# Operand steps at the two pass changes of an expert stage, moved behind the next unit's weight parts, and a larger filling budget at one point

## The chip, the cores and the metric

The kernel runs on one core of a Trainium2 chip. The metric is the time of one execution on the device in microseconds (us); shorter is better. Engines are named as in the profile: PE (matrix), PEld (its weight loads), DVE (vector), ACT (scalar), POOL (GpSimd), SP (issues the DMAs). Each engine works through its own instructions in the order in which the program wrote them.

## What is computed

Three stages follow one another; the output of each is the input of the next.

```python
attn_out = _attn_ref(q, k, v, phi)            # batch 4, 8 heads, 576 positions, 64 wide; 32 memory slots
x = attn_out.transpose(0, 2, 1, 3).reshape(2304, 512)
# second stage, d_ff = 2048
h = x @ w_in
x = (h * np.clip(h + 3.0, 0.0, 6.0) / 6.0) @ w_out
# third stage, the experts: E = 4, F = 1024
p = domain_probs / (domain_probs.sum(-1, keepdims=True) + 1e-09)
for e in range(E):
    h = np.maximum(x @ w1[e], 0.0)
    out += p[:, e:e + 1] * (h @ w2[e])
```

## The kernel before

**Number format.** Each float32 operand of a large product is held as two fp32r parts, `hi` (an ACT cast) and `lo` (a DVE subtraction of `hi` from the source). A product is three matmuls, hi·hi, hi·lo and lo·hi (`PASSES`). The second matmul of such a triple is the first that reads the `lo` part of the operand that is streamed, the third the first that reads the `lo` of the other.

**Before the expert stage.** Attention and the second stage are ordered by a planner (`Plan`), which runs until about 394 us of the trace. The change reaches it in one place only: the operand steps of the first token pair (`x_ops(0)`) are part of its plan, as a chain in the order of the list that `x_ops` returns.

**The expert stage** is written out by hand, at the end of `body`. The 2304 tokens are six tiles of 384; a pass `p` (0 to 2) takes two tiles. In a pass, chunk `c` (0 to 7) is one expert and half of its 1024 hidden columns; `n = 8p + c` counts 24 chunks. For a chunk, `unit(n, 0)` and `unit(n, 1)` compute the hidden activations of both tiles, 256 columns each, and `second(n, 1)` and `second(n, 0)` multiply them by the second weights of the expert, in three blocks of 128 tokens each, and add the result to `oacc` on DVE (line 961; line 959 in a pass's first chunk). In a pass's last chunk each `oacc` block is stored by a DMA.

**A unit** (`m = 2n + u`) does its 2×2 block product with seven products instead of eight, so it needs sums of the blocks of both sides: of the weights and of the tokens. The products run on PE in the order b, a, c, d, a, c, d (the second a, c and d add to the PSUM bank of the first, and are called a', c', d' here), six matmuls of 128x384 each. After the first b, ACT copies the bank (`p6`, line 914). DVE then forms `u2` from bank a and `p6`, `u4` from bank c and `u2`, and so on (line 905). So a' cannot start until `u2` has read bank a, nor c' until `u4` has read bank c. ACT applies relu (line 878), DVE the `lo` of the result (line 879).

**Weight parts.** For each unit a DMA brings a raw tile `u_raw`. Its steps, in order: casts `hi0`, `hi3` (ACT), `lo0`, `lo3` (DVE), four sums in place in the raw tile `s1`, `s3`, `s2`, `s4` (POOL, lines 326 to 335), then casts `hi2`, `hi1` of the summed blocks, and `lo2`, `lo1`. In the rows below W16_1 is part 1 of unit 16. Product b reads part 1, a part 0, c part 2, d part 2; a' part 0, c' part 1, d' part 3. The second weights have steps `w2hi` and `w2lo`, four of each per chunk (w2_8_3 is part 3 of chunk 8); `second` uses them in the order 0, 2, 3, 1.

**Token operands.** For each pass, `x_ops(p)` makes seven operands from the two token tiles: X11, X22, X21 are blocks, XT1 to XT4 differences. That is seven ACT casts of 128x768 (line 683), four DVE subtractions in place (line 689) and seven DVE `lo` steps (line 686). They overwrite the operands of the pass before, so they come after the last unit of that pass. Product b reads XT2 (xop4), a X11 (xop0), c XT1 (xop3), d XT3 (xop5), a' X21 (xop1), c' X22 (xop2), d' XT4 (xop6).

**What sets the order.** All these preparing steps stand in one list, `todo`, in a fixed order with marks called gaps. At given points the stage takes steps from its front:

```python
    def fill(t):            # takes steps until t us of vector work are used, or until a gap
    def need(key):          # takes steps until the one named has been taken
```

In a unit, `step(0.6)` stands after products b and a, and `step(0)` after the others; `second` calls `fill(1.9)` after each of its six blocks. Only DVE steps count against the budget, at fixed costs (0.6 for a 512 wide `lo`, 0.86 for an operand step); casts, sums and loads cost nothing there. A wait of one step holds everything behind it on its engine. At the two pass changes (after chunks 7 and 15, called seams here) the 18 operand steps are inserted at the front of `todo` before the second products of the old pass's last chunk.

Of the kernel before, what the change touches and what calls it, by code (L numbers as in the profile page):

```python
# [17 lines left out]
B, H, S, D = 4, 8, 576, 64  # L18
# [108 lines left out]
def body(ctx: ExitStack, tc: tile.TileContext, phiT, kv, qT, w_in, w_out, w1, w2, dp, out):  # L127
# [19 lines left out]
    at = ExitStack()  # L147
# [10 lines left out]
    def bank(name):  # L158
        return ps_w.tile([P, 512], F32, tag="h", name=name)
# [421 lines left out]
    for t in range(NTT):  # L581
        p, r = t * TW, []
        while p < (t + 1) * TW:
            b, s0 = divmod(p, S)
            n = min(S - s0, (t + 1) * TW - p)
# [79 lines left out]
    X11, X21, X22, XT1, XT2, XT3, XT4 = range(7)  # L665
    xop = {}

    def x_tile(k):
        if k not in xop:
            pool, tag = {X11: (0, "x0"), X21: (0, "x1"), X22: (0, "x2"), XT1: (0, "x3"), XT3: (wip, "wia"),  # L670
                         XT2: (keep_a, "attnT0"), XT4: (keep_a, "attnT1")}[k]
            xop[k] = (pool or late["x"]).tile([P, 2, 2, TW], F32R, tag=tag, name=f"xop{k}")
        return xop[k]

    def x_ops(p):

        a, b = acc[2 * p] if 2 * p in acc else None, acc.get(2 * p + 1)
        B11, B21 = (lambda: acc[2 * p][:, 0:2]), (lambda: acc[2 * p][:, 2:4])
        B12, B22 = (lambda: acc[2 * p + 1][:, 0:2]), (lambda: acc[2 * p + 1][:, 2:4])
        v = nc.vector.tensor_tensor  # L680

        def hi(k, src):
            nc.scalar.copy(x_tile(k)[:, 0], src())

        def lo(k, src):
            v(out=x_tile(k)[:, 1], in0=src(), in1=x_tile(k)[:, 0].bitcast(F32), op=ALU.subtract)

        def sub(out, x, y):
            v(out=out(), in0=x(), in1=y(), op=ALU.subtract)

        H = lambda k, src: (f"xhi{k}", "A", 750, partial(hi, k, src))
        L = lambda k, src: (f"xlo{k}", "V", 860, partial(lo, k, src))
        D = lambda k, out, x, y: (f"xt{k}", "V", 860, partial(sub, out, x, y))
        return [H(X11, B11), H(X22, B22), H(X21, B21), L(X11, B11), L(X22, B22), D(1, B11, B12, B11),
                D(3, B12, B22, B12), D(2, B22, B22, B11), H(XT1, B11), H(XT2, B22), H(XT3, B12), L(X21, B21),
                L(XT1, B11), L(XT2, B22), L(XT3, B12), D(4, B21, B21, B22), H(XT4, B21), L(XT4, B21)]

    def plan_ffn():
        nu = [(c, b) for c in range(NC1) for b in range(B)]
# [37 lines left out]
        for name, eng, cost, fn in x_ops(0):  # L737
            op((name,), eng, cost, fn, *prev)
            prev = [(name,)]
# [21 lines left out]
    todo, made = [], set()  # L761
# [4 lines left out]
    def go():  # L766
        key, t, ok, fn = todo.pop(0)
        assert ok(), key
        fn()
        made.add(key)  # L770
        return t

    def fill(t):
        some = False
        while todo and t > 0 and todo[0][2]():
            if todo[0][0] == "gap":
                todo.pop(0)
                if some:
                    break
            else:  # L780
                t -= go()
                some = True

    def need(key):
        while key not in made:
            if todo[0][0] == "gap":
                todo.pop(0)
            else:
                go()
# [79 lines left out]
    def flush(keep):  # L869
        while len(late_lo) > keep:  # L870
            late_lo.pop(0)()

    def h_tile(n, f, half, src):

        k = h_free.pop(0)
        h = hpool.tile([P, 2, TW], F32R, tag=f"h{k}", name=f"h{n}_{f}_{half}")
        hts[n, f, half] = h, k
        nc.scalar.activation(h[:, 0], src, AF.Relu)  # L878
        late_lo.append(lambda: nc.vector.scalar_tensor_tensor(out=h[:, 1], in0=src, scalar=0.0, in1=h[:, 0].bitcast(F32),
                                                              op0=ALU.max, op1=ALU.subtract))  # L880

    def unit(n, u):
        m = 2 * n + u
        W = units[m]
        bk = {}
        tmp = {}

        def tmp_tile(name, tag):
            tmp[name] = wip.tile([P, TW], F32, tag=tag, name=f"{name}_{m}")
            return tmp[name]  # L890

        def prod(b, k, o, x, first, last):
            if first:
                bk[b] = bank(f"p{b}")[:, 0:TW]
            for kt in range(2):
                for i, (xx, y) in enumerate(PASSES):
                    nc.tensor.matmul(bk[b], W[k][0][:, xx, o, kt * P:(kt + 1) * P], xop[x][:, y, kt],  # L897
                                     start=first and kt == 0 and i == 0, stop=kt == 1 and i == 2,
                                     skip_group_check=not first)

        def c_tile(tag):
            return rawp.tile([P, TW], F32, tag=tag, name=f"{tag}_{m}", bufs=2)

        def add_to(out, b, x):
            nc.vector.tensor_tensor(out=out, in0=bk[b], in1=x, op=ALU.add)  # L905
            return out

        def step(t):
            flush(1)
            fill(t)  # L910

        need(("lo1", m))
        prod("b", 1, 0, XT2, True, True)
        nc.scalar.copy(tmp_tile("p6", "wi0"), bk["b"])  # L914
        step(0.6)
        need(("lo0", m))
        prod("a", 0, 0, X11, True, False)
        add_to(tmp_tile("u2", "wi1"), "a", tmp["p6"])
        step(0.6)
        need(("lo2", m))  # L920
        prod("c", 2, 0, XT1, True, False)
        add_to(tmp_tile("u4", "wi2"), "c", tmp["u2"])
        step(0)
        prod("d", 2, 1, XT3, True, False)
        h_tile(n, u + 2, 1, add_to(c_tile("cy"), "d", tmp["u4"]))
        step(0)
        prod("a", 0, 1, X21, False, True)
        h_tile(n, u, 0, bk["a"])
        step(0)
        prod("c", 1, 1, X22, False, True)  # L930
        h_tile(n, u, 1, add_to(c_tile("cx"), "c", tmp["u2"]))
        step(0)
        need(("lo3", m))
        prod("d", 3, 0, XT4, False, True)
        h_tile(n, u + 2, 0, add_to(c_tile("cx"), "d", tmp["u2"]))
        step(0)
        for k, (_, t) in units.pop(m).items():
            (free_half if k == 3 else free_slots).append(t)

    def second(n, half):  # L940
# [26 lines left out]
        if half == 0:  # L967
            for i in range(4):
                free_slots.append(w2s.pop((n, i))[1])

    for n in range(last_n + 1):
        p, c = divmod(n, NCE)
        unit(n, 0)
        unit(n, 1)
        if c == NCE - 1 and p + 1 < NP:
            flush(0)
            for name, eng, cost, fn in reversed(x_ops(p + 1)):
                todo.insert(0, ((name, p + 1), cost / 1e3 if eng == "V" else 0, yes, fn))
        second(n, 1)
        second(n, 0)  # L980
        if c == NCE - 1 and p + 1 < NP:
            need((f"xlo{XT4}", p + 1))
# [33 lines left out]
```

## Time and profile before

| | |
|---|---|
| median of 3 runs | 1158.57 us (1158.21 to 1161.49) |
| the profiled execution | 1160.18 us, its span 1158.40 us |
| PE, PEld busy | 97%, 89% |
| DVE, ACT, POOL busy | 71%, 40%, 13% |
| mean granted TensorE clock | 0.994 of full speed |
| expert stage | from 394.2 us of the span to its end |
| HBM traffic | 83.66 MB read, 4.72 MB written |

Times in the rows are microseconds from the start of the span. A row of the timeline is one instruction or several of the same form in a row (xN), with its start and its length; what stands in brackets is the idle time of the engine before it, and what ended that. The end of a matmul is modelled, so of PE the starts are compared. The span is 1.78 us shorter than the execution's own time, and that execution is 1.61 us above the median of the runs.

### The profile page before, as it was taken

How to read it: one execution, taken by the hardware profiler on the slowest of the kernel's cores; microseconds unless marked ns; L12 is line 12 of the kernel's file. 1: busy time of each engine (PE TensorE's matmuls, PEld its weight loads, DVE VectorE, ACT ScalarE, POOL GpSimd, SP SyncE). 2: the span in 40 equal slices, each digit the busy share in tenths (PEclk: the TensorE clock that was granted, in tenths of full speed). 3: DMA queues.
4: the chain of work that ended last, by engine and by line, in shares of the span. 5: the costliest groups of instructions: out<-in, count | busy, mean ns of one | idle time of the engine just before them, and what ended most of it. 6: DMA issues, size and time to landing. Idle time of an engine off the chain costs nothing. (4 is left out here: it accounts for less than half of the span.)

```text
span 1158.4 us, 16603 instructions
## 1 busy us (share of the span) xinstructions
PE 1123.4 (97%) x6488; PEld 1027.2 (89%) x6488; DVE 821.6 (71%) x1510; ACT 463.4 (40%) x918; POOL 150.3 (13%) x200
## 2 busy tenths in 40 slices
PE   4899999999999999999999899999999899999998
PEld 3799999999999989999999799999999799999997
DVE  6999899974568577666667766666667766666664
ACT  2666654433344333333333343333334433333321
POOL 0000000000011023211121222222210222222210
PEclk9999999999999999999999999999999999999999
DMA  9832231210000032221111321222220222221201
GB/s 362 296 112 97 77 106 57 90 37 1 1 19 1 11 105 86 73 74 56 64 63 54 110 91 55 73 73 74 73 74 28 100 91 73 73 72 56 73 1 55
DMA packets 31167, 89.46 MB, mean 77 GB/s; under 512 B 2928, under 2 KB 2928, under 8 KB 30576
## 3 DMA queue, kind: packets, MB, share of 16 engines
q1 hardware_dynamic: 31088, 88.39, 22.6%
q8 instruction: 51, 0.84, 0.3%
q14 instruction: 28, 0.23, 0.1%
HBM read 83.66 MB, written 4.72 MB: 76 GB/s over the span
## 5 line engine op out<-in xcount | busy, mean ns | idle before, releaser
L953 PE MATMUL po<-w,h 128*128 128x512 f32 x1728 | 396.8, 390 | 1.4 <-DVE w L355 1.4
L953 PEld LDWEIGHTS po<-w,h 128*128 128x128 f32 x1728 | 323.9, 188 | 68.2 <-DVE w L355 1.8
L648 PE MATMUL pacc<-g,w 128*128 128x384 f32 x1152 | 213.9, 337 | 0.9 <-DVE g L372 0.9
L648 PEld LDWEIGHTS pacc<-g,w 128*128 128x128 f32 x1152 | 198.9, 188 | 8.0 <-issue 5.9
L961 DVE SCALAR_TENSOR_TENSOR oacc<-po,pr,oacc 128x512 f32<-128x512 f32 x126 | 94.3, 748 | 113.6 <-PE po L953 113.6
L326 POOL TENSOR_TENSOR u_raw<-u_raw 128x256 f32<-128x256 f32 x48 | 36.2, 755 | 954.1 <-DVE pair L323 690.8
L320 ACT CAST W<-u_raw 128x512 fp32r<-128x512 f32 (+1 forms) x160 | 87.5, 599 | 155.0 <-POOL u_raw L329 127.3
L897 PE MATMUL pa<-xop,W 128*128 128x384 f32 x576 | 116.5, 336 | 7.2 <-DVE u L905 7.2
L622 PE MATMUL ph<-attnT,u 128*128 128x384 f32 (+1 forms) x768 | 121.3, 306 | 0.1
L622 PEld LDWEIGHTS ph<-attnT,u 128*128 128x128 f32 x768 | 112.4, 190 | 5.9 <-DVE g L372 1.7
L897 PE MATMUL pc<-xop,W 128*128 128x384 f32 x576 | 116.7, 337 | 0.0
L897 PEld LDWEIGHTS pa<-xop,W 128*128 128x128 f32 x576 | 102.1, 189 | 7.8 <-DVE u L905 7.8
L897 PEld LDWEIGHTS pc<-xop,W 128*128 128x128 f32 x576 | 102.5, 190 | 0.1
L323 DVE TENSOR_TENSOR W<-u_raw,W 128x512 fp32r<-128x512 f32 (+1 forms) x160 | 97.5, 661 | 1.2 <-ACT W L320 0.9
L878 ACT ACTIVATE h<-cx 128x384 fp32r<-128x384 f32 x96 | 50.5, 526 | 79.1 <-DVE cx L905 79.1
L369 ACT CAST g<-t 128x384 fp32r<-128x384 f32 x96 | 49.4, 514 | 78.5 <-PE pacc L648 69.7
L372 DVE TENSOR_TENSOR g<-t,g 128x384 fp32r<-128x384 f32 x96 | 53.1, 555 | 38.3 <-ACT g L369 38.1
L914 ACT COPY p<-pb 128x384 f32<-128x384 f32 x48 | 23.1, 481 | 141.8 <-PE pb L897 141.5
L897 PE MATMUL pd<-xop,W 128*128 128x384 f32 x384 | 77.7, 337 | 0.0
L628 ACT ACTIVATE t<-ph,three 128x384 f32<-128x384 f32 x96 | 55.9, 582 | 52.9 <-DVE g L372 44.0
L897 PEld LDWEIGHTS pd<-xop,W 128*128 128x128 f32 x384 | 68.4, 190 | 0.0
L355 DVE TENSOR_TENSOR w<-w2raw,w 128x512 fp32r<-128x512 f32 x96 | 65.1, 703 | 0.0
(92 smaller groups left out, 1204.9 us busy)
## 6 DMA issues: line engine op xcount, KB each, us to landing
u_raw<-in_w SPq DMA_DIRECT2D x48, 512.0 KB, 3.2
w2raw<-in_w SPq DMA_DIRECT2D x48, 512.0 KB, 3.4
raw<-in_w_in SPq DMA_DIRECT2D x16, 512.0 KB, 4.0
kv<-in_kv SPq DMA_DIRECT2D x16, 512.0 KB, 7.7
raw<-in_w_out SPq DMA_DIRECT2D x16, 512.0 KB, 3.3
q<-in_qT SPq DMA_DIRECT2D x4, 1152.0 KB, 6.8
out_y<-oacc SPq DMA_DIRECT2D x18, 256.0 KB, 2.0
phi<-in_phiT SPq DMA_DIRECT2D x4, 576.0 KB, 8.6
```

The source lines that it names most:

```text
L320: nc.scalar.copy(w[:, 0], r()[:, slice(*parts[k])])
L323: v(out=W[k][0][:, 1], in0=r()[:, slice(*parts[k])], in1=W[k][0][:, 0].bitcast(F32), op=ALU.subtract)
L355: nc.vector.tensor_tensor(out=w[:, 1], in0=w2raw[n, q // 2][:, q % 2], in1=w[:, 0].bitcast(F32), op=ALU.subtract)
L369: nc.scalar.copy(hi, src)
L372: nc.vector.tensor_tensor(out=lo, in0=src, in1=hi.bitcast(F32), op=ALU.subtract)
L622: nc.tensor.matmul(ps[:, o:o + m], uts[c, b][:, x, hq, i * P:(i + 1) * P], attnT[b][:, y, hq, s0:s0 + m], start=(k == 0), stop=(k == 5))
L628: nc.scalar.activation(t, st["ph", n], AF.Relu, bias=three, scale=1.0)
L648: nc.tensor.matmul(pacc[j][:, 0:TW], w[:, x, j * P:(j + 1) * P], g[:, y], start=(i == 0 and k == 0), stop=(i == NI - 1 and k == 2))
L878: nc.scalar.activation(h[:, 0], src, AF.Relu)
L897: nc.tensor.matmul(bk[b], W[k][0][:, xx, o, kt * P:(kt + 1) * P], xop[x][:, y, kt], start=first and kt == 0 and i == 0, stop=kt == 1 and i ...
L953: nc.tensor.matmul(ps, hts[n, i, half][0][:, x, j * P:(j + 1) * P], w2s[n, i][0][:, y], start=(i == 0 and k == 0), stop=(i == 1 and k == 2))
L961: nc.vector.scalar_tensor_tensor(out=o, in0=ps, scalar=sc, in1=o, op0=ALU.mult, op1=ALU.add)
```

## The change

Four edits, all in the expert stage but for the list that the planner also uses:

- In `x_ops` the operand XT2 is made before XT1 (cast and `lo`), and the fourth subtraction and the cast of XT4 come before the `lo` of XT3.
- In a unit, the point after product b takes `step(1.2)` instead of `step(0.6)`.
- One `fill(0.1)` stands ahead of the stage's first unit.
- At a seam the 18 operand steps are inserted not at the front of `todo` but behind the step `s4` of unit 2n + 3, if that is still in the list: behind the last weight parts of the next chunk's first unit, and the first parts and the POOL sums of its second unit.

```diff
@@ x_ops
         return [H(X11, B11), H(X22, B22), H(X21, B21), L(X11, B11), L(X22, B22), D(1, B11, B12, B11),
-                D(3, B12, B22, B12), D(2, B22, B22, B11), H(XT1, B11), H(XT2, B22), H(XT3, B12), L(X21, B21),
-                L(XT1, B11), L(XT2, B22), L(XT3, B12), D(4, B21, B21, B22), H(XT4, B21), L(XT4, B21)]
+                D(3, B12, B22, B12), D(2, B22, B22, B11), H(XT2, B22), H(XT1, B11), H(XT3, B12), L(X21, B21),
+                L(XT2, B22), L(XT1, B11), D(4, B21, B21, B22), H(XT4, B21), L(XT3, B12), L(XT4, B21)]
@@ unit
         nc.scalar.copy(tmp_tile("p6", "wi0"), bk["b"])
-        step(0.6)
+        step(1.2)
         need(("lo0", m))
@@ the stage's loop
+    fill(0.1)
     for n in range(last_n + 1):
         p, c = divmod(n, NCE)
         unit(n, 0)
         unit(n, 1)
         if c == NCE - 1 and p + 1 < NP:
             flush(0)
-            for name, eng, cost, fn in reversed(x_ops(p + 1)):
-                todo.insert(0, ((name, p + 1), cost / 1e3 if eng == "V" else 0, yes, fn))
+
+            at = max([0] + [k + 1 for k, x in enumerate(todo) if x[0] == ("s4", 2 * n + 3)])
+            todo[at:at] = [((name, p + 1), cost / 1e3 if eng == "V" else 0, yes, fn) for name, eng, cost, fn in x_ops(p + 1)]
         second(n, 1)
         second(n, 0)
```

**DVE at the first seam, beginning of the second products of chunk 7.** The first row is the accumulation of the first of their six blocks. Before:

```order
L961 SCALAR_TENSOR_TENSOR oacc1_4437<-po_6391,pr_105,oacc1_4437 128x512
L686 TENSOR_TENSOR xop0_3815<-acc2_1331,xop0_3815 128x768
L686 TENSOR_TENSOR xop2_3838<-acc3_1555,xop2_3838 128x768
L689 TENSOR_TENSOR acc2_1331<-acc3_1555,acc2_1331 128x768
L961 SCALAR_TENSOR_TENSOR oacc1_4437<-po_6412,pr_105,oacc1_4437 128x512
L689 TENSOR_TENSOR acc3_1555<-acc3_1555 128x768
```

and now:

```order
L961 SCALAR_TENSOR_TENSOR oacc1_4439<-po_6392,pr_105,oacc1_4439 128x512
L323 TENSOR_TENSOR W16_1_6323<-u_raw16_6132,W16_1_6323 128x512
L323 TENSOR_TENSOR W17_0_6325<-u_raw17_6185,W17_0_6325 128x512
L323 TENSOR_TENSOR W17_3_6327<-u_raw17_6185,W17_3_6327 128x256
L686 TENSOR_TENSOR xop0_3815<-acc2_1331,xop0_3815 128x768
L961 SCALAR_TENSOR_TENSOR oacc1_4439<-po_6422,pr_105,oacc1_4439 128x512
L686 TENSOR_TENSOR xop2_3838<-acc3_1555,xop2_3838 128x768
L689 TENSOR_TENSOR acc2_1331<-acc3_1555,acc2_1331 128x768
```

Three `lo` steps of units 16 and 17 now stand ahead of all operand steps (a fourth, of W16_2, has gone into unit 15); POOL's four sums of unit 17 wait for the last of the three.

**DVE at the same seam, from the fourth accumulation on, to the `u2` of unit 16** (the rows with `po` are accumulations four to six). Before:

```order
L961 SCALAR_TENSOR_TENSOR oacc0_4509<-po_6451,pr_105,oacc0_4509 128x512
L689 TENSOR_TENSOR acc2_1331<-acc2_1331,acc3_1555 128x768
L686 TENSOR_TENSOR xop6_4077<-acc2_1331,xop6_4077 128x768
L323 TENSOR_TENSOR W16_2_6330<-u_raw16_6132,W16_2_6330 128x512
L961 SCALAR_TENSOR_TENSOR oacc0_4509<-po_6470,pr_105,oacc0_4509 128x512
L323 TENSOR_TENSOR W16_1_6332<-u_raw16_6132,W16_1_6332 128x512
L323 TENSOR_TENSOR W17_0_6334<-u_raw17_6199,W17_0_6334 128x512
L323 TENSOR_TENSOR W17_3_6336<-u_raw17_6199,W17_3_6336 128x256
L961 SCALAR_TENSOR_TENSOR oacc0_4509<-po_6500,pr_105,oacc0_4509 128x512
L355 TENSOR_TENSOR w2_8_2_6496<-w2raw8_1_6201,w2_8_2_6496 128x512
L355 TENSOR_TENSOR w2_8_3_6498<-w2raw8_1_6201,w2_8_3_6498 128x512
L323 TENSOR_TENSOR W17_2_6517<-u_raw17_6199,W17_2_6517 128x512
```

and now:

```order
L961 SCALAR_TENSOR_TENSOR oacc0_4509<-po_6461,pr_105,oacc0_4509 128x512
L686 TENSOR_TENSOR xop3_3970<-acc2_1331,xop3_3970 128x768
L689 TENSOR_TENSOR acc2_1331<-acc2_1331,acc3_1555 128x768
L686 TENSOR_TENSOR xop5_3980<-acc3_1555,xop5_3980 128x768
L961 SCALAR_TENSOR_TENSOR oacc0_4509<-po_6480,pr_105,oacc0_4509 128x512
L686 TENSOR_TENSOR xop6_4065<-acc2_1331,xop6_4065 128x768
L961 SCALAR_TENSOR_TENSOR oacc0_4509<-po_6500,pr_105,oacc0_4509 128x512
L355 TENSOR_TENSOR w2_8_2_6496<-w2raw8_1_6187,w2_8_2_6496 128x512
L355 TENSOR_TENSOR w2_8_3_6498<-w2raw8_1_6187,w2_8_3_6498 128x512
L323 TENSOR_TENSOR W17_2_6517<-u_raw17_6185,W17_2_6517 128x512
L323 TENSOR_TENSOR W17_1_6519<-u_raw17_6185,W17_1_6519 128x512
L905 TENSOR_TENSOR u2_16_6542<-pa_6535,p6_16_6531 128x384
```

The operand steps now run up to the sixth accumulation, and W17_1 stands ahead of `u2` instead of behind it. On ACT the order at the seam is the same in both kernels but for the casts of XT1 and XT2: seven operand casts, two `w2hi`, the casts of W17_2, W17_1, W18_0 and `pair`, then the `p6` copy of unit 16.

**ACT at the start of the expert stage** (the first row is the last cast of the second stage; `p6_0` is the copy after the first product b). Before:

```order
L914 COPY p6_0_4284<-pb_4277 128x384
L320 CAST W1_2_4288<-u_raw1_2779 128x512
L320 CAST W1_1_4290<-u_raw1_2779 128x512
L351 CAST w2_0_0_4292<-w2raw0_0_2689 128x512
L351 CAST w2_0_1_4294<-w2raw0_0_2689 128x512
```

and now:

```order
L320 CAST W1_2_4279<-u_raw1_2779 128x512
L320 CAST W1_1_4281<-u_raw1_2779 128x512
L351 CAST w2_0_0_4283<-w2raw0_0_2689 128x512
L351 CAST w2_0_1_4285<-w2raw0_0_2689 128x512
L914 COPY p6_0_4294<-pb_4287 128x384
```

The four casts stand ahead of the copy. On DVE the `lo` steps of W1_2 and W1_1 now come before the `u2` of unit 0, those of w2_0_0 and w2_0_1 before the `u2` of unit 1, that of w2_0_2 right behind it, and that of w2_0_3 stays between the last two `lo` steps of the hidden activations of chunk 0.

Elsewhere the order on DVE changes in 19 odd units (5 to 15, 19 to 31, 35 to 45), where the `lo` of the next unit's part 2 now stands between `u2` and `u4`; it came from a point after a block of `second`. Units 0 to 3, 16, 17, 32 and 33 change as shown or in the like way, the other even units not at all. On SP, at a seam, the loads of the second next first unit (u_raw18) and of w2raw9_0 now stand behind the first of the six stores instead of behind the fifth.

## Rows read from the trace of the kernel before

**Rows 1.** The page, part 1: busy time, share of the span, instructions.

```profile
PE 1123.4 (97%) x6488; PEld 1027.2 (89%) x6488; DVE 821.6 (71%) x1510; ACT 463.4 (40%) x918; POOL 150.3 (13%) x200
```

**Rows 2.** Busy time by stretch; columns: stretch, length, five engines, PEclk, DMA share, GB/s.

```profile
654.70:658.30 3.60, 3.60 (x12) 3.60 (x13) 2.10 (x4) 1.01 (x2) 0.00 (x0) 0.53 0.43 146
...
700.00:800.00 100.00, 100.00 (x501) 90.26 (x500) 66.08 (x116) 33.89 (x69) 20.66 (x28) 1.00 0.21 69
```

**Rows 3.** Waits of PE from 400 us on: total us, times, longest us.

```profile
PE pa L897 <- DVE u L905: 7.2, 2, 3.6
PE pb L897 <- DVE W L323: 4.3, 3, 1.5
...
```

**Rows 4.** Timeline of PE, first seam: start, length, engine, line, tiles, form, count, idle before.

```profile
614.09 1.23 PE L897 MATMUL pb<-xop,W 128*128 128x384 f32 x6
...
645.04 0.51 PE L897 MATMUL pb<-xop,W 128*128 128x384 f32 x2
...
647.00 0.97 PE L897 MATMUL pb<-xop,W 128*128 128x384 f32 x4 [1.46 <-DVE W L323]
...
654.67 2.29 PE L897 MATMUL pa<-xop,W 128*128 128x384 f32 x6 [3.58 <-DVE u L905]
...
658.43 1.20 PE L897 MATMUL pd<-xop,pair 128*128 128x384 f32 x6
...
683.11 1.23 PE L897 MATMUL pb<-xop,W 128*128 128x384 f32 x6
```

**Rows 5.** Timeline of POOL, ACT and DVE in the longer wait.

```profile
648.02 0.74 POOL L326 TENSOR_TENSOR u_raw<-u_raw 128x256 f32<-128x256 f32 x1 [33.02 <-DVE W L323]
...
652.21 1.14 ACT L320 CAST W<-u_raw 128x512 fp32r<-128x512 f32 x2 [1.65 <-POOL u_raw L335]
...
654.06 0.56 DVE L905 TENSOR_TENSOR u<-pa,p 128x384 f32<-128x384 f32 x1 [2.46 <-ACT p L914]
```

**Rows 6.** Timeline of DVE at the first seam, from the first accumulation.

```profile
631.64 0.75 DVE L961 SCALAR_TENSOR_TENSOR oacc<-po,pr,oacc 128x512 f32<-128x512 f32 x1 [1.06 <-PE po L953]
632.31 1.82 DVE L686 TENSOR_TENSOR xop<-acc,xop 128x768 fp32r<-128x768 f32 x2
...
634.04 0.95 DVE L689 TENSOR_TENSOR acc<-acc,acc 128x768 f32<-128x768 f32 x1
...
634.91 0.74 DVE L961 SCALAR_TENSOR_TENSOR oacc<-po,pr,oacc 128x512 f32<-128x512 f32 x1
...
646.27 1.62 DVE L323 TENSOR_TENSOR W<-u_raw,W 128x512 fp32r<-128x512 f32 x3
...
647.80 0.75 DVE L961 SCALAR_TENSOR_TENSOR oacc<-po,pr,oacc 128x512 f32<-128x512 f32 x1
...
650.59 1.00 DVE L323 TENSOR_TENSOR W<-u_raw,W 128x512 fp32r<-128x512 f32 x1
```

**Rows 7.** Timeline at the start of the expert stage: first unit, `second`, next chunk.

```profile
394.20 1.20 PE L897 MATMUL pb<-xop,W 128*128 128x384 f32 x6
...
395.44 0.48 ACT L914 COPY p<-pb 128x384 f32<-128x384 f32 x1 [6.53 <-PE pb L897]
...
410.40 1.08 PE L953 MATMUL po<-w,h 128*128 128x512 f32 x4
...
411.54 1.89 DVE L355 TENSOR_TENSOR w<-w2raw,w 128x512 fp32r<-128x512 f32 x3
...
412.88 15.70 PE L953 MATMUL po<-w,h 128*128 128x512 f32 x68 [1.39 <-DVE w L355]
...
428.41 1.23 PE L897 MATMUL pb<-xop,W 128*128 128x384 f32 x6
```

**Rows 8.** Timeline in unit 15: ACT casts, DVE u4, PE c'.

```profile
623.07 1.97 ACT L320 CAST W<-u_raw 128x512 fp32r<-128x512 f32 x4
...
624.72 0.56 DVE L905 TENSOR_TENSOR u<-pc,u 128x384 f32<-128x384 f32 x1 [0.43 <-PE pc L897]
...
626.60 1.20 PE L897 MATMUL pc<-xop,W 128*128 128x384 f32 x6
```

## The prediction

> **What bounds the kernel now.** I read the page first, then PE's waits, then its timeline. PE is busy 97% of the span [rows 1], and in a stretch in the middle of a pass it is busy all the time at the full clock [rows 2]. There the work of the other engines is hidden, and moving it can only lose. So what matters is where PE stands still. From 400 us on it waits in three kinds of places: for `u2` (two times, 3.6 us), for the `lo` of a weight part (three times, 1.5 us) [rows 3], and once for a second weight [rows 7].
>
> An undisturbed chunk takes 30.95 us, from the first product b at 614.09 to that at 645.04. The chunk behind the first seam takes 38.07, to 683.11 [rows 4]. **A seam costs 7.12 us**, in three parts. First, b of unit 16 stops after two matmuls until the `lo` of W16_1 is there. Second, a' starts at 654.67. From 647.00 on, four matmuls of b and a, c, d were left; a product takes 1.04 (from d' at 658.43 to 683.11 are 24.68, less 72 matmuls at 15.53/68 = 0.228 of rows 7, over eight products). So a' was due at 647.00 + 0.69 + 3.12 = 650.8, and is 3.9 late [rows 4, 7]. Third, the clock: behind that wait the granted clock is 0.53, which is the lower level of 1.2 GHz, for 3.6 us [rows 2], and a' and c' take 658.43 − 654.67 = 3.76 instead of 2.08: 1.68 [rows 4]. The first wait is 7.12 less the others, about 1.5. The waits of rows 3 count two of the long kind, so the second seam is the same.
>
> The long wait is a chain over three engines [rows 5]. POOL's sums for unit 17 start only at 648.02, because the vector steps that they wait for lay behind all operand steps. ACT's casts of the summed blocks wait for them until 652.21, and the `p6` copy of unit 16 stands behind these casts. `u2` waits for the copy, a' for `u2`.
>
> At the entry, the chunk from 394.20 to 428.41 takes 34.21, **3.26 us** too long: b of unit 1 waits for W1_1 (the third of its kind in rows 3), the first `second` for w2_0_2 [rows 7]. All that can be won is 2 × 7.12 + 3.26 = 17.5 us.
>
> **The change part by part.** Nothing is removed or added, 18 operand steps per seam and some `lo` steps change places.
>
> *Entry.* The four casts ahead of the first `p6` copy fall into 6.53 us in which ACT waited [rows 7]; at 0.57 each (two in 1.14, rows 5) they need 2.3, and cost nothing. W1_1 is then ready before unit 0 ends, and b of unit 1 does not wait. Of the second weights only the `lo` of w2_0_3 stays behind the unit. In the times of the old run, where `second` starts at 410.40, that step would start at 411.54 [rows 7] and end 0.67 later, at 412.2; its first reader is the eighth matmul, due at 410.40 + 7 × 0.228 = 412.0. A wait of 0.25 is left. **Gain 3.0.**
>
> *Seam.* The weight parts go first, so W16_1 is there ten microseconds early. POOL's sums start right behind W17_3, at about 631.64 + 0.67 + 1.53 + 0.15 = 634.0 instead of 648.02, and ACT no longer waits for them at the end. What comes late instead is DVE itself, which now has all 18 operand steps in the stretch where `u2` is due. I add up its row from the first accumulation at 631.64 to `u2` of unit 16, by start-to-start times [rows 6, 7]: six accumulations at 0.67 (631.64 to 632.31), seven operand `lo` at 0.865 (two from 632.31 to 634.04), four subtractions at 0.87 (to 634.91), the trio W16_1, W17_0, W17_3 at 1.53 (646.27 to 647.80), and w2_8_2, w2_8_3, W17_2, W17_1 at 0.61 each: 4.02 + 6.06 + 3.48 + 1.53 + 2.44 = 17.5. The accumulations do not add waits, because DVE is behind PE from the second on. `u2` would start at 649.2 and end 0.56 later, at 649.7. a' is due at 645.04 + 4 × 1.04 = 649.2. So even undisturbed a' waits 0.55.
>
> To that comes POOL beside DVE. A `lo` step beside the sums took 1.00 [rows 6]; alone it takes 0.67 (three in 1.89 less two paces of 0.61, rows 7). POOL's four sums need 4.2 us (648.02 to 652.21, rows 5), so until 638.2, and three or four of the operand steps lie beside them: 3 × 0.33 = 1.0 more, 1.3 at most. An accumulation reads PSUM and was not longer (0.75, begun at 647.80, beside the sum at 648.02). I take 1.0, **a wait of 1.6 at a'** in place of 7.12; its ends are 0.55 and 1.9.
>
> A rule of the Trainium skill ("SBUF — State Buffer", Who interferes with whom) speaks against so small a price: a vector instruction with two inputs in SBUF and a GpSimd instruction that reads SBUF exclude each other, and the second to issue is blocked until the first has finished. By it the wait at a' would be 3.5 where by the row it is 1.6; the row shows 0.33 per step, less than half a sum, so it speaks for the smaller. The larger is a rival below.
>
> Is anything else later than that? The operands are ready in time: XT2, read by b at 645.0, is finished after three accumulations, the trio, four `lo` and three subtractions, at 641.3 + 1.0; XT1, XT3 and XT4 follow with 3 us and more to spare before c, d and d'. The `p6` copy stands behind XT4's cast, which can start when the fourth subtraction ends, at 631.64 + 2.68 + 1.53 + 4.33 + 3.48 + 1.0 = 644.7, and six casts (two in 1.14 and four in 1.97, rows 5, 8). With as much for XT4's cast as for a `lo`, and half a microsecond for the copy, it ends near 649.2, a microsecond before `u2` can start at 650.2. The loads of u_raw18 and w2raw9_0 pass four stores on SP and only come earlier. The clock: a wait of 1.5 came before 647.00, and c and d behind it ran at full pace; behind one of 3.9 the clock fell [rows 2, 4]. 1.6 is next to the former, so I put the clock at nothing; its price is 1.68.
>
> *Steady units.* In 19 odd units a `lo` of 0.61 now stands between `u2` and `u4`. DVE waited 0.43 there anyway; `u4` would end at about 625.5 instead of 625.28, and c' starts at 626.60 [rows 8]. Its cast is the first of four on ACT from 623.07. Cost nothing, covered by over a microsecond. The step that leaves `second` leaves a place where DVE waited for PE: no gain either. XT2 before XT1 in the plan of the second stage lies beside a PE that is busy throughout: nothing.
>
> *Sum.* 3.0 + 2 × (7.12 − 1.6) = 14.0. The profiled execution took 1160.18 (span 1158.40 and 1.78 around it); the seams are the same in every run, so I take the sum from the median, 1158.57: **1144.5 us.**
>
> **The rivals.**
> - *No Pool contention*, or DVE catches up: the wait is 0.55 or nothing. Time 1158.57 − 3.0 − 2 × 6.57 = 1142.4, at the least 1158.57 − 17.5 = 1141.1. For it: an accumulation beside a sum was not slowed. Against: the 1.00.
> - *The clock falls at the shorter wait*: 2 × 1.68 more, 1147.9. For it: at its upper end the new wait lies between the two that the rows show. Against: 1.6 is close to the one that cost nothing.
> - *Each sum holds DVE for its whole length*: 4 × 0.74 [rows 5] = 3.0 instead of 1.0, the wait is 3.5, about that of the old kernel, and the clock falls with it: 5.2 per seam, 1158.57 − 3.0 − 2 × 1.9 = 1151.8. Against: 0.33 in the row. This is the rule of the Trainium skill's "SBUF — State Buffer", Who interferes with whom, carried through.
> - *The seam doesn't gain what it should*, because `p6` stays late: the casts are held by something that the sums hid, say u_raw18, whose cast is also ahead of the copy. Only the entry is won: 1155.6. Against: its load now starts 14 us earlier.
> - *Slower*: c' waits in the 19 odd units, if the `lo` ahead of `u4` gets its cast late. It decides from a start of that `lo` at 626.60 − 0.56 − 0.61 = 625.4, 1.2 us later than the row allows now. If it came 1.0 later than that, 19 × 1.0: 1163.5. Against: the cast needs sums that were finished in the chunk before, and nothing in rows 8 waits for them.
>
> **How the numbers follow.** The forecast 0.55, no contention 0.13, clock 0.16, whole sums 0.06, seam without gain 0.07, slower 0.03. The range leaves out the last three: from 1141.5, within the first rival, to 1150, above the clock case. About 0.3% (3.5 us) is what a measurement here can tell from no change: faster 0.90, same 0.07, slower 0.03.
>
> **What would show it.** In the profile after: product b at both seams without a wait; one wait at each a', of 1 to 2 us, ended by `u2`, with ACT's copy done before; POOL's sums 14 us earlier; the clock at 1.00 through both seams; the chunk behind a seam 32 to 33 us long, the first one 31.2. A wait at c' in odd units, or at b for XT2, would make it wrong; so would a clock of 0.5 behind a'.

## The result, and the profile after

| | before | after |
|---|---|---|
| median (runs of both on one chip) | 1158.39 us (1157.46 to 1161.49, 4 runs) | 1146.94 us (1143.60 to 1149.20, 4 runs) |
| the profiled execution, its span | 1160.18, 1158.40 us | 1144.87, 1143.10 us |
| start of the expert stage (first product b) | 394.20 us | 392.60 us |
| from there to the end of the span | 764.2 us | 750.5 us |
| chunk 0; chunks 8 and 16; any other chunk | 34.21; 38.07, 38.09; 30.95 us | 31.31; 32.66, 32.67; 30.95 us |

The ratio of after to before is 0.9894 (95% interval 0.9859 to 0.9930): **11.5 us less by the medians**, in the range forecast and 2.4 us above the time forecast. Two later series of both kernels gave 0.9877 (0.9852 to 0.9903) and 0.9896 (0.9874 to 0.9918), by the medians 14.1 and 11.9 us less. The expert stage of the two profiled executions differs by 764.2 − 750.5 = 13.7 us, and three chunks hold that: 2.90 at the entry, 5.41 and 5.42 at the seams. The rest of the difference between single executions lies ahead of that stage (last section).

Page of after, part 1 (against [rows 1]), and all waits of PE from 390 us on (against [rows 3]; columns: what waited, for what, total us, times, longest us):

```profile
PE 1118.4 (98%) x6488; PEld 1023.3 (90%) x6488; DVE 837.9 (73%) x1510; ACT 462.4 (40%) x918; POOL 166.2 (15%) x200
```

```profile
PE pa L897 <- DVE u L905: 2.8, 2, 1.4
```

Instruction counts are the same. Of the waits, those of `pb` and `po` are gone, and the two at a' are 1.4 instead of 3.6. POOL and DVE are busy for 16 us longer each with the same work. On DVE one group holds it, the `lo` of the second weights (columns: busy us, mean ns of one | idle time ahead of them):

```profile
L355 DVE TENSOR_TENSOR w<-w2raw,w 128x512 fp32r<-128x512 f32 x96 | 82.2, 877 | 0.0
```

Its mean was 703 ns before. It is 887 in e1_entry and 688 in e2_seam (below), so it comes with `step(1.2)`: where a `lo` has gone ahead between `u2` and `u4`, this step lies beside POOL's sums. It costs no time, as the chunks between the seams show.

PE at the first seam, timeline of after (against [rows 4]):

```profile
640.54 1.23 PE L897 MATMUL pb<-xop,W 128*128 128x384 f32 x6
...
643.68 1.20 PE L897 MATMUL pd<-xop,W 128*128 128x384 f32 x6
...
646.30 1.32 PE L897 MATMUL pa<-xop,W 128*128 128x384 f32 x6 [1.41 <-DVE u L905]
647.45 1.23 PE L897 MATMUL pc<-xop,W 128*128 128x384 f32 x6
...
673.20 1.05 PE L897 MATMUL pb<-xop,W 128*128 128x384 f32 x5
```

Product b runs through. a' was due 1.04 after d, at 644.72, and starts at 646.30: 1.58 late. (The profile counts 1.41 of that as idle, because the modelled end of d lies later than its pace; the text calls the first lateness and the second idle time.) c' follows 1.15 later where 1.04 is a product's pace. Together they are 1.69 of the 32.66 − 30.95 = 1.71 that the seam still costs. The clock at both seams (columns: stretch, length, five engines, granted clock, DMA share, GB/s):

```profile
640.00:650.00 10.00, 8.59 (x49) 8.09 (x48) 9.30 (x17) 5.40 (x11) 0.00 (x0) 1.00 0.48 164
...
889.00:899.00 10.00, 8.59 (x48) 8.06 (x47) 9.30 (x16) 5.11 (x11) 0.00 (x0) 1.00 0.52 173
```

It stays at 1.00, the level of 2.4 GHz, where it was 0.53 behind the longer wait [rows 2].

DVE, POOL and ACT at the same seam, timeline of after (against [rows 5, 6]):

```profile
627.14 0.75 DVE L961 SCALAR_TENSOR_TENSOR oacc<-po,pr,oacc 128x512 f32<-128x512 f32 x1 [1.05 <-PE po L953]
627.81 1.62 DVE L323 TENSOR_TENSOR W<-u_raw,W 128x512 fp32r<-128x512 f32 x3
...
629.56 1.33 POOL L326 TENSOR_TENSOR u_raw<-u_raw 128x256 f32<-128x256 f32 x1 [21.52 <-DVE W L323]
...
630.97 2.32 POOL L329 TENSOR_TENSOR u_raw<-u_raw 128x256 f32<-128x256 f32 x1
631.74 0.95 DVE L689 TENSOR_TENSOR acc<-acc,acc 128x768 f32<-128x768 f32 x1
632.72 1.38 DVE L689 TENSOR_TENSOR acc<-acc 128x768 f32<-128x768 f32 x1
633.37 1.34 POOL L332 TENSOR_TENSOR u_raw<-u_raw 128x256 f32<-128x256 f32 x1
634.03 0.74 DVE L961 SCALAR_TENSOR_TENSOR oacc<-po,pr,oacc 128x512 f32<-128x512 f32 x1
634.69 0.94 DVE L689 TENSOR_TENSOR acc<-acc,acc 128x768 f32<-128x768 f32 x1
634.79 1.44 POOL L335 TENSOR_TENSOR u_raw<-u_raw 128x256 f32<-128x256 f32 x1
635.55 2.36 DVE L686 TENSOR_TENSOR xop<-acc,xop 128x768 fp32r<-128x768 f32 x2
...
637.84 0.74 DVE L961 SCALAR_TENSOR_TENSOR oacc<-po,pr,oacc 128x512 f32<-128x512 f32 x1
...
644.05 0.47 ACT L914 COPY p<-pb 128x384 f32<-128x384 f32 x1
...
645.69 0.55 DVE L905 TENSOR_TENSOR u<-pa,p 128x384 f32<-128x384 f32 x1
```

The parts go first, POOL starts at 629.56 (counted from the first accumulation, 14.0 us earlier than before), the copy of p ends at 644.52, and `u2` starts at 645.69 with no idle time before it: DVE itself is late now. Its row from the first accumulation to `u2` takes 645.69 − 627.14 = 18.55.

The entry, timeline of after (against [rows 7]), and unit 15 (against [rows 8]):

```profile
393.84 0.48 ACT L914 COPY p<-pb 128x384 f32<-128x384 f32 x1 [4.44 <-PE pb L897]
...
407.16 16.91 PE L953 MATMUL po<-w,h 128*128 128x512 f32 x72
408.30 0.68 DVE L355 TENSOR_TENSOR w<-w2raw,w 128x512 fp32r<-128x512 f32 x1
```

```profile
620.30 0.55 DVE L905 TENSOR_TENSOR u<-pc,u 128x384 f32<-128x384 f32 x1
...
622.10 1.20 PE L897 MATMUL pc<-xop,W 128*128 128x384 f32 x6
```

ACT still waited 4.44 us ahead of the copy, so its casts were free, and the 72 matmuls of `second` run as one group. In unit 15 `u4` ends at 620.85 with c' at 622.10.

### The profile page after: what moved, and what is told of

Read it like the earlier page. It is cut to its first block, busy times and chain, and to the rows that moved or that the text cites. A ratio compares the mean times of both kernels' runs of the same rounds, so it can differ in the third digit from the quotient of the medians.

```text
span 1143.1 us, 16606 instructions
## 1 busy us (share of the span) xinstructions
PE 1118.4 (98%) x6488; PEld 1023.3 (90%) x6488; DVE 837.9 (73%) x1510; ACT 462.4 (40%) x918; POOL 166.2 (15%) x200
## 4 chain that ended last, share of the span: by engine, by line
PE 96%; DVE 3%; DMA 0%; ACT 0%; issue 0%; ACTq 0%
PE po L953 34%; PE pacc L648 17%; PE ph L622 9%; PE pa L897 9%; PE pc L897 9%; PE pd L897 8%; PE pb L897 4%; PE psc L458 1%; PE pu L605 1%; PE pk L432 1%; PE pe L503 0%; PE pa L415 0%; DMA raw<-in_w_in 0%; DVE mx L390 0%; DVE cy L230 0%; DVE W L323 0%
## 5 line engine op out<-in xcount | busy, mean ns | idle before, releaser
L355 DVE TENSOR_TENSOR w<-w2raw,w 128x512 fp32r<-128x512 f32 x96 | 82.2, 877 | 0.0
```

What stands on the lines that cost most here:

```text
L355: nc.vector.tensor_tensor(out=w[:, 1], in0=w2raw[n, q // 2][:, q % 2], in1=w[:, 0].bitcast(F32), op=ALU.subtract)
```

## The experiments

**What is compared.** The start of the expert stage differs by several us between executions, so the text goes by two lengths inside one trace: a chunk (start of its first b to that of the next) and the stage (first b to the end of the span). "Seams" are chunks 8 and 16. The medians of the table can't be set against one another as they stand: those of before and after come from one series, the others from three later ones, in which before read 1161.79 (a1, e1, e2, e5), 1161.14 (e3, e4, e6_ahead, e7) and 1161.37 (a2, e6_again, e8).

| kernel | median us | stage us | chunk 0 | seams |
|---|---|---|---|---|
| before | 1158.39 | 764.2 | 34.21 | 38.07, 38.09 |
| after | 1146.94 | 750.5 | 31.31 | 32.66, 32.67 |
| a1_after, a2_after | 1147.68, 1149.46 | 750.5, 750.5 | 31.3, 31.32 | 32.67, 32.67; 32.66, 32.65 |
| e1_entry | 1158.30 | 761.0 | 31.31 | 37.44, 38.47 |
| e2_seam | 1151.05 | 754.0 | 34.26 | 32.92, 32.96 |
| e3_no_sums (one time) | 1142.29 | 748.7 | 31.30 | 31.82, 31.82 |
| e4_old_list | 1149.13 | 752.8 | 31.30 | 34.59, 33.05 |
| e7_longer (one time) | 1150.26 | 751.7 | 31.33 | 33.25, 33.23 |
| e8_first_unit (one time) | 1153.09 | 758.7 | 31.3 | 36.75, 36.73 |
| e5_late | 1151.43 | 752.9 | 30.93 | 34.87, 33.31 |
| e6_ahead, e6_again | 1143.79, 1145.27 | 746.6, 746.6 | 30.92 | 30.95, 30.95 |

### The two halves apart

**a1_after: the changed kernel again.**

> The changed kernel again. Theory A (three separate pieces: the start of the expert stage 3.0, each seam 7.12 less a wait of 1.6): chunks 8 and 16 take 32.6 us, chunk 0 takes 31.3, time 1143 to 1149. Its executions spread over 5.6 us (1143.6 to 1149.2). Theory C: in some of them the clock falls behind the 1.6 wait at a', 1.7 per seam, and the slow ones have a mean clock lower by about 0.003 (3.4 us at half speed lost of 1143). Theory D: the spread comes from ahead of the expert stage, and the seams always keep the full clock.

The span was 1147.2, 4.1 longer than in the first trace, and the first b came at 396.70 instead of 392.60: the same 4.1. The stage, its chunks and its two waits were the same, as theory D says.

**e1_entry: the entry alone**, with the operand steps where they were.

```diff
-        step(0.6)          # behind product b
+        step(1.2)
...
+    fill(0.1)
     for n in range(last_n + 1):
```

> The kernel before with only the larger budget after product b and the filling ahead of the first unit; the operand steps stay at the front of the list at the seams. Theory A: chunk 0 takes 31.3 instead of 34.2 (3.0 won); the seams keep the late copy, and as one lo step goes into the last unit of the old pass, b waits 0.6 less: 6.5 instead of 7.1 per seam. Time 1158.5 - 3.0 - 1.2 = 1154.3. Rival: the larger budget itself repairs the seams (b and a' on time): 1143 to 1146.

The ratio to before was 0.9972 (0.9952 to 0.9992). Chunk 0 is that of the full change. At the seams b now waits almost not at all, and little is won by it: the first gains 38.07 − 37.44 = 0.63, the second loses 0.38 (waits of PE from 390 us on; POOL and ACT at the first seam; granted clock behind each wait at a'):

```profile
PE pa L897 <- DVE u L905: 8.4, 2, 4.2
PE pb L897 <- DVE W L323: 0.4, 2, 0.2
```

```profile
642.83 0.73 POOL L326 TENSOR_TENSOR u_raw<-u_raw 128x256 f32<-128x256 f32 x1 [34.87 <-DVE W L323]
...
648.35 0.47 ACT L914 COPY p<-pb 128x384 f32<-128x384 f32 x1
```

```profile
648.00:653.00 5.00, 3.54 (x12) 3.54 (x13) 3.08 (x6) 1.80 (x5) 0.00 (x0) 0.67 0.48 165
902.00:909.00 7.00, 5.46 (x17) 5.46 (x18) 4.18 (x8) 2.43 (x6) 0.00 (x0) 0.52 0.35 127
```

b waits 1.3 less, but a' waits 0.6 longer, since u2 still waits for the copy of p. The copy starts 21.30 after the first accumulation (at 627.05) instead of 653.56 − 631.64 = 21.92: the 0.62 is the one `lo` that no longer stands ahead of POOL's sums, and it is what the first seam gains. The second seam should have gained as much. There the waits are the same, but the clock stayed low through three products instead of two, and the chunk is 38.47 − 37.44 = 1.03 longer; that was not foreseen.

**e2_seam: the seams alone.**

```diff
-        step(1.2)          # behind product b
+        step(0.6)
...
-    fill(0.1)
```

> The change without the larger budget and without the filling ahead of the first unit: only the new place and order of the operand steps. Theory A: chunk 0 stays at 34.2; at a seam the row of DVE up to u2 has the same steps in number (the lo of W16_2 comes in, that of W17_1 goes out), so a' waits 1.6 and the chunk takes 32.6, as in the full change: 1158.5 - 2 x 5.5 = 1147.5 in executions like those of the kernel before. Rival: the larger budget is needed at the seams, a' or b waits 0.6 or more longer: 1149 or more.

The ratio to before was 0.9904 (0.9866 to 0.9942). Chunk 0 is that of before (34.26), the seams gain 5.15 and 5.13. The stage gains of the two halves, 3.2 and 10.2, add up to 13.4 of the 13.7 of the full change: the pieces hardly depend on one another. The 0.27 that a seam takes more here is DVE's: its row from the first accumulation to `u2` takes 650.14 − 631.32 = 18.82 against 18.55. As many steps stand in it, but W16_2 stands there ahead of the sums and W17_1 behind `u2`, and the sums meet other steps.

**e4_old_list: the old order of the operand list.**

```diff
-                ... H(XT2, B22), H(XT1, B11), H(XT3, B12), L(X21, B21),
-                L(XT2, B22), L(XT1, B11), D(4, B21, B21, B22), H(XT4, B21), L(XT3, B12), L(XT4, B21)]
+                ... H(XT1, B11), H(XT2, B22), H(XT3, B12), L(X21, B21),
+                L(XT1, B11), L(XT2, B22), L(XT3, B12), D(4, B21, B21, B22), H(XT4, B21), L(XT4, B21)]
```

> The full change with the old list of operand steps (XT1 before XT2, the lo of XT3 before the fourth subtraction). Theory A: the same steps stand ahead of u2; XT2 is ready one step (0.87) later, at 642 where b starts at 645 in the old times, and the copy of p6 comes 0.87 later but still 0.3 before u2 can start: chunks 8 and 16 within 0.2 of 32.67, time as the full change. Rival (the new order of the list carries part of the gain): b or a' waits longer, 33.5 or more.

The list is worth more than expected: a' comes 0.38 us later at both seams (the second takes 33.05 against 32.67). The timeline shows where: the fourth subtraction comes one step later, and DVE then waits for the cast between it and the `lo` of XT4. At the first seam the clock fell as well (0.57 from 651 to 655 us), for 1.5 more:

```profile
646.61 0.96 DVE L686 TENSOR_TENSOR xop<-acc,xop 128x768 fp32r<-128x768 f32 x1 [0.30 <-ACT xop L683]
...
651.15 2.10 PE L897 MATMUL pa<-xop,W 128*128 128x384 f32 x6 [1.80 <-DVE u L905]
```

### What carries the gain, and what is left

**e8_first_unit: the first unit ahead of the operand steps, the sums behind them.**

```diff
-            at = max([0] + [k + 1 for k, x in enumerate(todo) if x[0] == ("s4", 2 * n + 3)])
+            at = max([0] + [k + 1 for k, x in enumerate(todo) if x[0] == ("lo1", 2 * n + 2)])
```

> The changed kernel, except that at a seam the token operands' steps go in behind the first unit's accumulation alone and not behind the second unit's too: unit 16 (and 32) of the next chunk goes ahead of them, while the second unit's two parts, the last part's accumulation and with them the Pool sums of the next chunk stay behind the steps. Theory: what is worth the gain is that the Pool sums, the casts behind them and the copy of p start before the operands' steps; with the steps ahead of the second unit all of these come late, a' waits for u2 about as long as in the kernel before (3.6 us) and the seam's chunks take 36 to 38 us against 32.7 in the full change; a first b does not wait. Rival: the first unit alone ahead of the steps carries the gain, the sums are quick enough afterwards: 32.5 to 34 us a seam chunk. Total by the theory about 1154, by the rival about 1147.

b does not wait, and yet a seam takes 36.75: 1.3 of the 5.4 is won. Timeline of the first seam of this kernel:

```profile
642.22 0.74 POOL L326 TENSOR_TENSOR u_raw<-u_raw 128x256 f32<-128x256 f32 x1 [34.15 <-DVE W L323]
...
647.75 0.47 ACT L914 COPY p<-pb 128x384 f32<-128x384 f32 x1
...
648.25 0.56 DVE L905 TENSOR_TENSOR u<-pa,p 128x384 f32<-128x384 f32 x1 [0.51 <-ACT p L914]
...
648.87 1.45 PE L897 MATMUL pa<-xop,W 128*128 128x384 f32 x6 [3.94 <-DVE u L905]
```

It is the old chain again: late sums, late casts, late copy; here `u2` waits for the copy. So the early start of POOL's sums carries the larger part of the gain, and the early W16_1 does not. What is shown is that this chain costs the time. Whether it could also be cut elsewhere, by putting the copy ahead of the casts on ACT with the sums left late, was not tried.

**e3_no_sums: the changed kernel without the sums of units 17 and 33.** The eight sums are left out, so two weight parts of each of these units are not the right ones; only the times are of use.

```diff
+                if eng == "P" and m in (17, 33):
+                    fn = lambda: None
```

> The full change with POOL's four sums of units 17 and 33 left out, so that nothing runs on POOL beside the operand steps (two weight parts of these two units are then not the sums). Theory A (1.0 of the 1.6 at a' is POOL beside DVE): a' waits 0.6, chunks 8 and 16 take 31.6. Rival 1 (POOL costs DVE nothing in operand steps, the backlog is longer than added up): 32.67 as in the full change. Rival 2 (a sum holds DVE for its whole length): the wait of the full change would have to be 3.0 of POOL, and this one shows no wait at all, 30.95.

A seam takes 31.82, so the sums cost 32.67 − 31.82 = 0.85 of PE's time. a' was due at 643.91 and started at 644.64. DVE's row went from 626.32 to 644.03, 17.71 by the timeline, against 18.55 with the sums:

```profile
626.32 0.75 DVE L963 SCALAR_TENSOR_TENSOR oacc<-po,pr,oacc 128x512 f32<-128x512 f32 x1 [1.06 <-PE po L955]
...
631.91 0.96 DVE L689 TENSOR_TENSOR acc<-acc 128x768 f32<-128x768 f32 x1
632.78 0.74 DVE L963 SCALAR_TENSOR_TENSOR oacc<-po,pr,oacc 128x512 f32<-128x512 f32 x1
...
634.31 1.95 DVE L686 TENSOR_TENSOR xop<-acc,xop 128x768 fp32r<-128x768 f32 x2
636.17 0.74 DVE L963 SCALAR_TENSOR_TENSOR oacc<-po,pr,oacc 128x512 f32<-128x512 f32 x1
...
642.87 1.21 PE L899 MATMUL pd<-xop,W 128*128 128x384 f32 x6
644.03 0.55 DVE L907 TENSOR_TENSOR u<-pa,p 128x384 f32<-128x384 f32 x1
...
644.64 1.32 PE L899 MATMUL pa<-xop,W 128*128 128x384 f32 x6 [0.57 <-DVE u L907]
```

**e7_longer: one more `lo` ahead of `u2` at a seam.**

```diff
-        step(1.2)
+        step(1.7 if u == 0 and n > 0 and n % NCE == 0 else 1.2)
```

> The full change with one more lo step (0.61) ahead of u2 in the first unit behind a seam. Theory A: the wait at a' grows from 1.6 to 2.2, chunks 8 and 16 take 33.3. Theory C (the clock falls behind some waits between 1.7 and 3.9, not always): at this wait one or both of the seams may show a clock of 0.5 behind a' and a chunk of 35.0; without a fall at either, the two together take 2 x 0.6 more than in the full change.

A seam takes 33.25, so 0.58 more for a step of 0.61, and the clock did not fall behind the idle time of 2.0 at either seam. DVE's row sets a' step for step.

**e5_late: the steps of the seam's points behind `u2` and `u4`.** The next thing to try was thus to take steps out of that row: nothing behind b, 1.2 behind each of a and c, and no filling behind the last of the six blocks of the second products. At chunk 0 the point behind a takes 1.2 too.

```diff
-        step(1.2)                                   # behind b
+        seam = u == 0 and n > 0 and n % NCE == 0
+        step(0 if seam else 1.2)
...
-        step(0.6)                                   # behind a
+        step(1.2 if seam or n == 0 else 0.6)
...
-        step(0)                                     # behind c
+        step(1.2 if seam else 0)
...
-            fill(1.9)
+            fill(0 if half == 0 and j == 2 and c == NCE - 1 and p + 1 < NP else 1.9)
```

> The full change, and at a seam the four lo steps of w2_8_2, w2_8_3, W17_2, W17_1 stand behind u2 and u4 instead of ahead of u2; in chunk 0 the lo of w2_0_3 comes one point earlier. Theory A (a' waits for the backlog of DVE): 4 x 0.61 = 2.44 leave the row ahead of u2, more than the wait of 1.6, so a' does not wait, chunks 8 and 16 take 30.95 to 31.2, chunk 0 takes 31.0; 3.2 + 0.3 less than the change, span 1139.5 where the change has 1143. Rival (ACT's copy, not DVE, holds u2): the copy moves ahead of two casts only, a' still waits 1 us, 1142. Theory C: without a wait the clock never falls at a seam, and the slow executions are gone; theory D: they stay.

a' no longer waits, as expected, but the total did not follow: the ratio to before was 0.9906 (0.9878 to 0.9934), and the stage is 2.4 longer than after's. The filling had stopped at a gap of the list, and the `lo` of W17_1 was taken only when product b of the second unit needed it. PE's rows at that place, first and second seam, with the granted clock behind each:

```profile
651.21 0.97 PE L897 MATMUL pb<-xop,W 128*128 128x384 f32 x4 [2.08 <-DVE W L323]
...
652.02 1.59 PE L897 MATMUL pa<-xop,W 128*128 128x384 f32 x6
...
902.71 0.98 PE L897 MATMUL pb<-xop,W 128*128 128x384 f32 x4 [2.07 <-DVE W L323]
903.53 1.21 PE L897 MATMUL pa<-xop,W 128*128 128x384 f32 x6
```

```profile
652.00:656.00 4.00, 4.00 (x17) 4.00 (x16) 1.97 (x4) 1.52 (x3) 3.26 (x4) 0.58 0.41 131
...
902.00:906.00 4.00, 3.29 (x19) 3.30 (x20) 2.76 (x7) 1.52 (x3) 2.12 (x3) 1.00 0.44 129
```

A wait of the same length let the clock fall at one seam and not at the other; the fall cost 34.87 − 33.31 = 1.56.

**e6_ahead and e6_again: the same, with one more point.** Behind product d of the seam's unit two more steps are taken, so that W17_1 is there in time.

```diff
         h_tile(n, u + 2, 1, add_to(c_tile("cy"), "d", tmp["u4"]))
-        step(0)
+        step(1.2 if seam else 0)
```

> As the run with the four lo steps behind u2 and u4 at a seam, but W17_2 and W17_1 right behind the step that reads bank d, ahead of the hidden activations' lo steps, so that W17_1 is ready before b of unit 17. Theory A: then neither a' nor that b waits, chunks 0, 8 and 16 all take 30.95 to 31.2, the wait of the full change (1.72 per seam) and its 0.35 in chunk 0 are won: about 3.7 less than the full change, 1143.9 where it had 1147.7. Rival (the backlog of DVE only moves on, to bank c or d of unit 16 or to u2 of unit 17): chunk 8 keeps a wait of 0.6 or more, 1146.

The ratio to before was 0.9859 (0.9832 to 0.9886). All chunks take 30.92 to 30.95, and from 390 us on PE waits for nothing; at the first seam it is busy throughout (columns as above):

```profile
648.00:652.00 4.00, 4.00 (x25) 4.00 (x24) 4.00 (x8) 2.36 (x5) 1.59 (x2) 1.00 0.40 131
```

Then this version and the change ran in one series on one chip.

> The changed kernel as it is, for comparison with e6_again on one chip. Chunks at the seams 32.7 us and a wait of u2 at a' of 1.4 us in each; the median between 1144 and 1149, moved by the start of the expert stage (392.6 to 396.7 us so far) and by nothing behind it. If the wait of 1.4 us should let the clock fall in some executions, a seam's chunk would read 34 us or more with a granted clock of 0.5 behind the wait.

> The version with no wait at a seam (steps at the seam's points moved behind u2 and u4, and one step more behind d) again, on the same chip as the change. By the lengths of the chunks it should stand 3.8 us below it (two seams of 32.67 against 30.95 us, and chunk 0 of 31.31 against 30.95): a ratio to the change of about 0.9967, some 1142 to 1144 if the change reads 1146 to 1148. Rival: the difference lies within what the start of the expert stage adds to single executions (4 us), and the medians do not separate them; then the chunks alone decide, again 30.95 us for all of them, with no TensorE wait behind 390 us.

a2_after gave 1149.46 (1146.48 to 1150.45), e6_again 1145.27 (1141.22 to 1146.51), six runs each: 4.2 us less, a ratio of the medians of 0.9964. The fastest run of the change is 0.03 below the slowest of the other, and the stages differ by 750.5 − 746.6 = 3.9. It beats both kernels; what PE still waits for lies ahead of 390 us.

## Why the prediction was right

**What bounds the kernel.** PE's gaps at three places were the whole of it. With all of them closed (e6_ahead) the stage is 764.2 − 746.6 = 17.6 us shorter; the prediction had 17.5 to win.

**Entry, 3.0.** Measured 34.21 − 31.31 = 2.90, in after and in e1_entry alone. The wait left at w2_0_3 was put at 0.25; its `lo` ends at 408.98 where its reader was due at 407.16 + 7 × 0.228 = 408.76, and chunk 0 is 0.36 above a chunk without waits, which is the 0.1 that is missing. The casts ahead of the copy cost nothing, as said.

**Seam, a wait of 1.6 in place of 7.12.** Measured: a' 1.58 late, the chunk 1.71 longer than others. Its parts:

- DVE's row without the sums was summed to 17.5 and a wait of 0.55. e3_no_sums shows 17.71 and a' 0.73 late. The 0.18 is small change: the pair at 634.31 takes 1.86 where two at 0.865 were counted, and the subtraction ahead of 631.91 a tenth more than 0.87, while other steps took a little less.
- POOL beside DVE was put at 1.0; e3_no_sums shows 0.85. The two misses nearly cancel. **The sum was right, its picture was not**: it had three steps at 0.33 each. In the rows of after, set against those of e3_no_sums, two places pay: the subtraction at 632.72 takes 1.31 to the next row (0.87 without sums) and the pair at 635.55 2.29 (1.86), 0.44 and 0.43. The other two sums end beside an accumulation, which is not longer for it (0.74 at 634.03). POOL pays far more: its four sums take 6.43 instead of 2.96. The rows show who waits for whom: the last three sums end 0.60 or 0.61 after the end of the subtraction that they meet (633.29, 634.71 and 636.23 behind 632.69, 634.10 and 635.63), and the subtraction at 632.72 ends 0.81 after the end of the sum that it meets.
- The rival in which each sum holds DVE for its whole length would have made the wait 3.5; it was 1.58. The rule of the Trainium skill behind it ("SBUF — State Buffer", Who interferes with whom), that the second of the two to issue is blocked, fits these rows as far as they go: the sums at 630.97 and 634.79 stretch to 2.32 and 1.44 beside subtractions, and the same section's statement that a vector instruction with at most one SBUF input does not contend agrees with the 0.74 of the accumulation, which has one input in PSUM. What failed was carrying it through to 4 × 0.74, as if DVE were always the second.
- POOL's four sums were taken to last 4.2; they lasted 636.23 − 629.56 = 6.67. That cost nothing: the casts behind them were done when the copy's turn came.
- The copy of p was to be ready a microsecond before `u2`; it was, by 645.69 − 644.52 = 1.17. e8_first_unit shows the price if it is not: 36.75 − 32.66 = 4.1 us a seam, the fall of the clock in it.

**The clock.** It stayed up in all six seams of the three traces of after, behind 1.40 to 1.41 of idle time. The reason given, that 1.6 is next to a wait which had cost nothing, was right with little to spare: behind 1.80 (e4_old_list) and 2.08 (e5_late) it fell in one seam of two. That rival had its chance for good reason.

**Steady units.** All chunks but three take 30.95, as before. c' in unit 15 has 622.10 − 620.85 = 1.25 to spare, so the slower case was far off. Not foreseen was that the `lo` of the second weights would meet POOL's sums there (877 ns instead of 703); that DVE waits in these chunks hid it.

**The total.** 14.0 were forecast, the stage gave 13.7. That the median stands 2.4 above the forecast is most likely a matter of which executions were drawn. With the stage and the 1.78 around the span taken off, the three runs that the forecast starts from began the stage at 392.2, 392.6 and 395.5, the four runs of after at 391.3, 392.6, 396.7 and 396.9. That takes the stage as equal in executions without a trace; it was, in the three traces of after. The thin step of the prediction is that it added its sum to a median of three runs as if all ahead of the stage were equal. A spread of some 5 us there stands nowhere in its working, and the range, drawn from the rivals, happened to be wide enough for it.

## What to carry to other kernels

In a list that one engine works off in order, put first what another engine's chain hangs on (here four sums on POOL and the casts behind them), and last what is only bulk on the engine itself; making the directly awaited part early won only 1.3 of 5.4 us alone. Then add up the new last engine's row, instruction by instruction from start-to-start times: that sum, with the price of POOL beside it, told the wait left over (1.6 against 1.58; each of its two parts was within 0.2) and which steps to move next. After each move ask what now stops the filling, since a step that nobody takes early comes back as a wait one product later.

## What was not expected of the hardware

**The clock behind a short wait is not the same twice.** Behind idle times of TensorE of 1.4 to 1.7 it stayed at 2.4 GHz in all eight seams traced, behind 2.0 in both; behind 1.80 and 2.08 it fell to 1.2 GHz in one of two seams of the same program; behind 3.6 to 4.2 in all six. A fall cost about 1.5 us by the lengths of the chunks, and in one case (e1_entry, second seam) by estimate 2.5. What decides between 1.8 and 2.1 stays open.

**The spread of the runs goes with the first 41 us.** There attention begins and the granted clock is at the lower level for a time that differs between executions. Stretches in after (first two rows) and in a2_after (last two), columns as above:

```profile
24.00:28.00 4.00, 2.46 (x28) 1.98 (x19) 3.00 (x6) 2.43 (x6) 0.00 (x0) 1.00 1.02 413
...
36.00:40.00 4.00, 4.00 (x64) 3.32 (x56) 3.95 (x9) 2.40 (x9) 0.00 (x0) 1.00 0.93 337
```

```profile
24.00:28.00 4.00, 4.00 (x27) 2.22 (x26) 1.95 (x2) 0.77 (x2) 0.00 (x0) 0.50 1.02 413
...
36.00:40.00 4.00, 3.26 (x29) 2.19 (x32) 3.92 (x10) 1.48 (x5) 0.00 (x0) 0.50 0.87 346
```

It is the same program. In the first the clock is low only in the eight microseconds between these rows, in the second from about 23 to 41 us, and its expert stage starts 397.29 − 392.60 = 4.7 later; the spans differ by the same 4.7. In all thirteen traces the start of the stage goes with the time at the lower level: 391.8 us after some 4 us of it, 392.5 to 392.7 after 8 in one piece (394.2 after 8 in two pieces, in before), 393.8 after 11, 396.6 to 397.3 after 18. The seams do not make the spread: e6_ahead, where PE waits for nothing from 390 us on, ran from 1139.73 to 1145.67. That the clock makes the difference was read from the traces, and no kernel was made to test it.
